# Top-k attention before two expert layers: the threshold sign takes its bias straight from the 24th maximum, and five of eight tiles are masked on VectorE instead of four

## The chip, the cores and the metric

The kernel runs on one core of one Trainium2 chip. The metric is the device time of one execution in microseconds (us); less is better. Engines are named as in the profile: PE is TensorE (PEld its weight loads), DVE is VectorE, ACT is ScalarE, POOL is GpSimd, SP is SyncE, which here only issues DMAs.

## What is computed

Attention over 4 batches, 8 heads, 576 positions and head size 64, of which each query keeps only its 32 largest scores; the result goes through a layer of three matrices with a maximum (512 to 768 to 512) and then through one of eight experts for each token (512 to 1024 to 512).

```python
scores = (1 / sqrt(64)) * q @ k.T
kth = np.partition(scores, -32, axis=-1)[..., -32:-31]
scores = np.where(scores >= kth, scores, -1e9)
attn = softmax(scores)          # exp of scores less their maximum, over their sum + 1e-9
x = (attn @ v)                  # 2304 tokens x 512
x = np.maximum(np.maximum(x @ w1, x @ w2), x @ w3) @ w_out
e = argmax(x @ w_gate, axis=1)  # one expert for each token, with its softmax weight
out[token] = weight * (np.maximum(x @ ew1[e], 0) @ ew2[e])
```

The change lies in the second and third line: how the 32nd largest score of a row is found, and how the smaller ones are dropped.

## The kernel before

The attention is cut into 144 tiles of 128 query rows by 576 scores, in 36 groups of four. The program is written out by hand in ticks: tick t holds one stage of each of some dozen tiles in flight, in a fixed order on each engine, and each engine works its own queue in that order. A tile n goes through these stages:

- PE multiplies q and k; ACT copies the scores to a tile `s`, scaled by 2^-68 (L899).
- DVE, tick n: the 8 largest of each sixth of a row (`c<-s`, L921, six instructions), then three rounds on these 48 candidates (L936 to L940). The last round leaves `T3`, whose last column is the row's 24th largest candidate. L946 multiplies this column by -(1 - 2^-21) and writes it to `bf`.
- ACT, tick n + 2: `g`, the sign of `s` plus `bf` (L968), written as an unsigned 16-bit number, with its row sum in `cnt` (how many scores lie above). Read as a half float, a 1 is 2^-24.
- POOL, tick n + 3: `f` = `s` - `g` (L974). The scores are far below 2^-24, so that those above the threshold become very small negative numbers.
- DVE, tick n + 4: the 8 largest of `f` (L983), which are the 25th to 32nd of the row. After the fourth tile of a group DVE works for all four: `hsel` from `cnt` (L989), a copy of the 24th into `y8` (L991), `heq`, a test for near ties (L992), then a product and a sum (L1012, L1013) that give `hkth`, the 32nd.
- The scores under `hkth` are then dropped in one of two ways. "Early" tiles: ACT makes a second sign against `hkth` (L1043), POOL subtracts it from `s` (L1046), and ACT's exponential `e` (L1052) gives 0 there. The others: ACT takes the exponential of all of `s`, and DVE masks `e` with s >= hkth (L1057, one instruction, whose inputs `s` and `e` both lie in SBUF).
- ACT rounds `e` to half (L1063), POOL takes the rest (L1067), a DMA transposes both, PE multiplies with v (L1086), DVE divides.

`early(n)` decides by the table `ZN`: with `ZN = (2,)` the third and fourth tile of each group are early, so that 72 tiles take each way. `let_in` makes the next POOL subtraction of `s` wait for the masks written out before it. At the end `st_verdict` counts rows without a valid `hkth` and rows with a near tie (`heq`); if any were found the whole kernel would be run again in a general form, which does not happen here.

Between these stages PE works on the two later layers with what the ticks leave: the list of work for each tick is fixed in the program. After the last tile the expert layers run on alone.

Of the kernel before, what the change touches and what calls it, by code (L numbers as in the profile page):

```python
# [7 lines left out]
F32 = mybir.dt.float32  # L8
F16 = mybir.dt.float16
I32 = mybir.dt.int32  # L10
U16 = mybir.dt.uint16
ACTF = mybir.ActivationFunctionType
ALU = mybir.AluOpType
AX = mybir.AxisListType
# [5 lines left out]
def kernel(  # L20
# [20 lines left out]
    P = 128  # L41
# [13 lines left out]

    DOWN = 2.0 ** -68
    LOW = -1.0e30
    UNIT_RATE, TAIL_RATE = 1.08, 2.0
    NEARLY, NPICK, NMIX, NS1 = 10, 2, 7, 8
    CAP, XA, NSL, NLD, NAHEAD = 1.2, 3, 10, 4, 4  # L60
    NSWAP, XLAG, KLAG, TSTOP, EARLY_RATE, LATE_RATE = 4, 2, 2, 140, 1.4, 1.8
    RANK_LAG = 1
    ZN, NFB, NGB = (2,), 2, 4
    WARM, ST = 4, 4
    ESC = 1.0 / (float(D) ** 0.5 * SC * SC * DOWN)
    LSC = 1.0 / (SC * SC)
# [28 lines left out]
    def attempt(ctx, general):  # L95
# [5 lines left out]
        tri16 = const.tile([P, P], F16, name="tri16")  # L101
        one = const.tile([P, 1], F32, name="one")
        NG = NTL // G
        bad = const.tile([P, 2], F32, name="bad")
        base = const.tile([P, NE], F32, name="base")
        ebase = const.tile([1, NE], F32, name="ebase")

# [21 lines left out]
        wg = const.tile([P, 2, KD, NE], F16, name="wg")  # L129

        def consts():
            nc.gpsimd.iota(iota32, pattern=[[0, G], [-2, 9]], base=2 * TOP - S, channel_multiplier=0,
                           allow_small_or_imprecise_dtypes=True)
            nc.gpsimd.iota(rev8, pattern=[[-1, NE]], base=NE, channel_multiplier=0,
                           allow_small_or_imprecise_dtypes=True)
            nc.gpsimd.iota(base, pattern=[[REG, NE]], base=0, channel_multiplier=0,
                           allow_small_or_imprecise_dtypes=True)
            nc.gpsimd.iota(ebase, pattern=[[REG, NE]], base=0, channel_multiplier=0,
                           allow_small_or_imprecise_dtypes=True)
            nc.vector.tensor_copy(out=viota, in_=iota32)  # L140
# [12 lines left out]
            nc.gpsimd.affine_select(out=tri16, in_=ones16, pattern=[[1, P]], compare_op=ALU.is_gt, fill=0.0,  # L153
                                    base=0, channel_multiplier=-1)
# [472 lines left out]
        with ExitStack() as p1:  # L627
# [28 lines left out]
            if not general:  # L656

                hsel = a_p.tile([P, NHS, G, 9], F16, name="hsel")
                hkth = a_p.tile([P, NG, G], F32, name="hkth")
                heq = a_p.tile([P, NG, G, 1], F16, name="heq")  # L660
            live = [0]

            def mm_tile():
# [4 lines left out]
            def freed():  # L668
                live[0] -= 1
# [207 lines left out]
                return go  # L877


            Sps, Ss, T1, T3, zz, bf, be, cnt, y8, kth, ff, ee, pt = ({} for _ in range(13))  # L880
            xhl, xrem, avt = {}, {}, {}

            def st_scores(n):
# [40 lines left out]
            def st_rounds(n):  # L924
# [14 lines left out]
                    lambda: nc.vector.match_replace(out=c, in_to_replace=t2, in_values=c2, imm_value=LOW),  # L939
                    lambda: nc.vector.max(out=T3[g][:, i], in_=c),  # L940
                ]
                if i == 0:
                    cnt[g] = sm_p.tile([P, G, 1], F32, tag="cnt", name="cnt")
                    bf[g] = sm_p.tile([P, G, 1], F32, tag="bf", name="bf")
                ops.append(None)
                ops.append(lambda: nc.vector.tensor_scalar(out=bf[g][:, i], in0=T3[g][:, i, 7:8], scalar1=-(1.0 - 2.0 ** -21),  # L946
                                                           scalar2=None, op0=ALU.mult))
                return chain(ops)

            def st_bias(g):  # L950
# [11 lines left out]
            def st_over(n):  # L962

                if general:
                    return
                g, i = divmod(n, G)
                gg[n] = wk_p.tile([P, S], U16, tag="g", name="g", bufs=NGB)
                nc.scalar.activation(out=gg[n], in_=Ss[n], func=ACTF.Sign, bias=bf[g][:, i], accum_out=cnt[g][:, i])  # L968

            def st_rest(n):  # L970
                if general:
                    return
                ff[n] = wk_p.tile([P, S], F32, tag="f", name="f", bufs=NFB)
                let_in(nc.gpsimd.tensor_tensor(out=ff[n], in0=Ss[n], in1=gg.pop(n).bitcast(F16), op=ALU.subtract))  # L974

            def st_next8(n):
                if general:
# [7 lines left out]
            def st_pick(g):  # L985

                if general:
                    return
                bulk.append(lambda: nc.vector.tensor_tensor(out=hsel[:, g % NHS], in0=viota,  # L989
                                                            in1=cnt[g].to_broadcast([P, G, 9]), op=ALU.is_equal))  # L990
                tail_bulk.append(lambda: nc.vector.tensor_copy(out=y8[g][:, :, 0:1], in_=T3[g][:, :, 7:8]))  # L991
                tail_bulk.append(lambda: nc.vector.scalar_tensor_tensor(  # L992
                    out=heq[:, g], in0=y8[g][:, :, 1:2], scalar=-1.0, in1=bf[g], op0=ALU.mult, op1=ALU.is_le))

            def st_kth(g):
                kt = sm_p.tile([P, G], F32, tag="kth", name="kth") if general else hkth[:, g]
                kth[g] = kt
                if general:
# [10 lines left out]
                        nc.vector.tensor_copy(out=kt[:, i:i + 1], in_=m8[:, 7:8])  # L1009
                    return chain([lambda i=i: search(i) for i in range(G)])  # L1010
                return chain([
                    lambda: nc.vector.tensor_tensor(out=y8[g], in0=hsel[:, g % NHS], in1=y8[g], op=ALU.mult),  # L1012
                    lambda: nc.vector.tensor_reduce(out=kt, in_=y8[g], axis=AX.X, op=ALU.add),  # L1013
                ])

            def st_verdict():

                hit = a_p.tile([P, NG * G], F16, name="hit")
                chain([
                    lambda: nc.vector.tensor_scalar(out=hit, in0=hkth.rearrange("p n g -> p (n g)"), scalar1=0.0,  # L1020
                                                    scalar2=None, op0=ALU.is_gt),
                    lambda: nc.vector.tensor_reduce(out=bad[:, 0:1], in_=hit, axis=AX.X, op=ALU.add),
                    lambda: nc.vector.tensor_reduce(out=bad[:, 1:2], in_=heq.rearrange("p n g e -> p (n g e)"),
                                                    axis=AX.X, op=ALU.add),
                    lambda: nc.vector.scalar_tensor_tensor(out=bad[:, 0:1], in0=bad[:, 0:1], scalar=-1.0,
                                                           in1=bad[:, 1:2], op0=ALU.mult, op1=ALU.add),
                ])

                def total():
                    ps = mm_tile()[0:1, 0:1]  # L1030
                    nc.tensor.matmul(out=ps, lhsT=one, rhs=bad[:, 0:1], start=True, stop=True)
                    after(1, lambda: chain([lambda: (nc.vector.tensor_scalar(
                        out=again, in0=ps, scalar1=float(P * NTL), scalar2=None, op0=ALU.add), freed())]))
                after(4, total)


# [737 lines left out]
```

## Time and profile before

| | |
|---|---|
| median of 3 runs | 921.35 us (921.21 to 921.8) |
| profiled execution | 916.4 us, span 914.7 us |
| busy share of the span | PE 81%, PEld 63%, DVE 82%, ACT 75%, POOL 65% |
| first and last mask on DVE (L1057) | starts at 73.5 and 676.6 us |
| mean granted TensorE clock | 0.964 |

Busy time is time in which at least one instruction of the engine was at work. On DVE an instruction starts before the one ahead of it has ended, so that the durations of single instructions add up to more than the busy time; where it matters the start-to-start time is taken instead, from the timeline.

### The profile page before, as it was taken

The numbers are of one execution on the slowest core, as the hardware profiler recorded it, in microseconds if no ns is written. First come the engines' busy times: TensorE is split into PE (matmuls) and PEld (weight loads), VectorE is DVE, ScalarE is ACT, GpSimd is POOL, SyncE is SP. The second block draws the span as 40 slices with busy tenths as digits, with TensorE's granted clock in tenths as the row PEclk, the third lists the DMA queues.
The fourth block names the chain that finished last, engine by engine and source line by source line (L and its number), as shares of the span: only waits on it lengthen the run. The fifth ranks groups of instructions, "written<-read, shape, count | busy, mean of one in ns | idle before, by whom it ended". The sixth has DMA issues, their size and how long they took to land.

```text
span 914.7 us, 29063 instructions
## 1 busy us (share of the span) xinstructions
PE 738.9 (81%) x10606; PEld 574.4 (63%) x10606; DVE 749.4 (82%) x3252; ACT 682.1 (75%) x1320; POOL 597.5 (65%) x554
## 2 busy tenths in 40 slices
PE   1111357888888799978988889989999999999993
PEld 0000236666665678757767687767987756687882
DVE  5999999999999899999998999999852426476661
ACT  4758899988998899899987889998862231566661
POOL 2556789898989699987877889879982220211110
PEclk9999977999899899999989999999999999999997
DMA  9872977886997998899999888897977469699280
GB/s 227 264 228 50 221 150 148 134 140 133 186 173 148 161 166 168 158 197 178 163 168 177 166 151 165 162 190 148 196 148 128 128 171 298 170 295 265 60 221 19
DMA packets 372162, 155.91 MB, mean 170 GB/s; under 512 B 331931, under 2 KB 348319, under 8 KB 372000
## 3 DMA queue, kind: packets, MB, share of 16 engines
q1 hardware_dynamic: 368128, 143.10, 76.3%
q0 software_dynamic: 3136, 9.46, 3.2%
q8 instruction: 87, 1.43, 0.7%
q10 hardware_dynamic: 736, 1.32, 0.5%
q14 instruction: 75, 0.61, 0.2%
HBM read 76.06 MB, written 16.67 MB: 101 GB/s over the span
## 4 chain that ended last, share of the span: by engine, by line
DVE 32%; issue 20%; PE 19%; POOL 11%; ACT 7%; DMA 7%; SPq 2%; POOLq 0%; DVEq 0%; ACTq 0%
PE mm L355 9%; DVE c L921 7%; DVE vec L983 4%; DVE e L1057 4%; POOL phl L1067 3%; POOL f L974 3%; PE av L1086 2%; POOL s L1046 2%; DVE a L1164 2%; DVE hl L746 1%; DMA st<-in_q_dram 1%; POOL out_dram L405 1%; ACT e L1052 1%; DVE c L937 1%; DVE c L939 1%
## 5 line engine op out<-in xcount | busy, mean ns | idle before, releaser
L355 PEld LDWEIGHTS <-W 128*128 128x128 f16 x4560 | 250.4, 100 | 22.7 <-issue 19.6
L355 PE MATMUL mm<-xT,W 128*128 128x128 f16 x3456 | 214.3, 224 | 16.0 <-DVE vl L746 4.8
L974 POOL TENSOR_TENSOR f<-s,g 128x576 f32<-128x576 f32 x144 | 184.4, 1281 | 34.5 <-ACT g L968 16.5
L1067 POOL TENSOR_TENSOR phl<-e,phl 128x576 f16<-128x576 f32 x144 | 189.0, 1313 | 8.7 <-ACT phl L1063 7.8
L921 DVE MAX8 c<-s 128x8 f32<-128x96 f32 x864 | 174.8, 243 | 3.7 <-ACT s L899 3.7
L892 PEld LDWEIGHTS <-qT 128*128 128x128 f16 (+1 forms) x640 | 56.2, 106 | 184.2 <-issue 149.1
L892 PE MATMUL S<-kt,qT 128*128 128x64 f16 (+3 forms) x320 | 60.3, 337 | 107.3 <-ACT s L899 92.1
L1052 ACT ACTIVATE e<-s,be 128x576 f32<-128x576 f32 x144 | 110.8, 769 | 23.8 <-POOL phl L1067 15.8
L1086 PE MATMUL av<-vh,pt 128*128 128x65 f16 (+3 forms) x1600 | 109.7, 199 | 15.1 <-DVE xn L1135 9.7
L983 DVE MAX8 vec<-f 128x8 f32<-128x576 f32 x144 | 108.9, 756 | 4.7 <-POOL f L974 2.0
L968 ACT ACTIVATE g<-s,bf 128x576 uint16<-128x576 f32 x144 | 111.0, 771 | 0.5 <-DVE bf L946 0.5
L1046 POOL TENSOR_TENSOR s<-s,g 128x576 f32<-128x576 f32 x72 | 92.7, 1287 | 25.4 <-DVE e L1057 24.4
L1086 PEld LDWEIGHTS <-pt 128*128 128x128 f16 (+3 forms) x2400 | 88.5, 102 | 28.0 <-issue 11.8
L899 ACT ACTIVATE s<-S 128x576 f32<-128x576 f32 x144 | 92.4, 642 | 17.9 <-PE S L892 17.7
L1063 ACT ACTIVATE phl<-e 128x576 f16<-128x576 f32 x144 | 97.3, 676 | 11.0 <-DMA pt<-phl 10.7
L1086 PE MATMUL av<-vl,pt 128*128 128x64 f16 (+3 forms) x800 | 99.3, 196 | 0.0
L461 DVE SCALAR_TENSOR_TENSOR W<-st,W 128x1024 f16<-128x1024 f32 x56 | 65.8, 1221 | 37.3 <-ACT W L460 31.8
L1057 DVE SCALAR_TENSOR_TENSOR e<-s,hkth,e 128x576 f32<-128x576 f32 x72 | 81.8, 1136 | 11.7 <-ACT e L1052 7.7
L892 PE MATMUL S<-kT,qT 128*128 128x512 f16 (+3 forms) x320 | 48.9, 295 | 18.8 <-ACT s L899 18.5
L1170 POOL TENSOR_TENSOR hhl<-a,hhl 128x384 f16<-128x384 f32 x36 | 37.0, 1027 | 33.4 <-ACT hhl L1169 31.9
L460 ACT ACTIVATE W<-st 128x1024 f16<-128x1024 f32 x56 | 55.6, 1046 | 1.8 <-DMA st<-in_moe_w_dram 1.8
L1043 ACT ACTIVATE g<-s,hkth 128x576 uint16<-128x576 f32 x72 | 55.2, 767 | 0.0
(233 smaller groups left out, 1566.6 us busy)
## 6 DMA issues: line engine op xcount, KB each, us to landing
st<-in_moe_w_dram SPq DMA_DIRECT2D x72, 512.0 KB
st<-in_moe_w_dram SPq DMA_DIRECT2D x28, 256.0 KB
raw<-in_moe_w_dram SPq DMA_DIRECT2D x12, 512.0 KB
st<-in_v_dram SPq DMA_DIRECT2D x16, 256.0 KB
hs<-he SPq DMA_DIRECT2D x16, 256.0 KB
hTe<-hs SPq DMA_DIRECT2D x8, 512.0 KB
st<-in_q_dram SPq DMA_DIRECT2D x15, 256.0 KB
qT<-qT SPq DMA_DIRECT2D x30, 128.0 KB
```

What stands on the lines that cost most here:

```text
L355: nc.tensor.matmul(out=ps[:, o * n:(o + 1) * n], lhsT=w(b, kk, c), rhs=x(a, kk), start=(kk == 0 and i == 0), stop=(kk == KD - 1 and i == 2))
L892: nc.tensor.matmul(out=ps[o:o + m, j, 0:(REM if j else NQ * P)], lhsT=qt[:, vv, hh, 0:m], rhs=kr[:, hh] if j else km[:, hh // HG, :, hh % HG],
L921: nc.vector.max(out=c[:, i * 8:(i + 1) * 8], in_=s[:, i * CW:(i + 1) * CW])
L968: nc.scalar.activation(out=gg[n], in_=Ss[n], func=ACTF.Sign, bias=bf[g][:, i], accum_out=cnt[g][:, i])
L974: let_in(nc.gpsimd.tensor_tensor(out=ff[n], in0=Ss[n], in1=gg.pop(n).bitcast(F16), op=ALU.subtract))
L983: bulk.append(lambda: nc.vector.max(out=y8[g][:, i, 1:9], in_=y))
L1046: let_in(nc.gpsimd.tensor_tensor(out=Ss[n], in0=Ss[n], in1=zz.pop(n).bitcast(F16), op=ALU.subtract))
L1052: nc.scalar.activation(out=e, in_=Ss.pop(n) if early(n) else Ss[n], func=ACTF.Exp, scale=ESC, bias=be[g][:, i])
L1057: masked.append(nc.vector.scalar_tensor_tensor(out=e, in0=Ss.pop(n), scalar=kth[g][:, i:i + 1], in1=e, op0=ALU.is_ge, op1=ALU.mult))
L1063: nc.scalar.activation(out=ph[:, 0, 0:S], in_=p, func=ACTF.Copy)
L1067: nc.gpsimd.tensor_tensor(out=ph[:, 1, 0:S], in0=p, in1=ph[:, 0, 0:S], op=ALU.subtract)
L1086: nc.tensor.matmul(out=av[o:o + m, i, 0:n], lhsT=t[0:kk, p * NCH + c, o:o + m], rhs=v_rows(x, b, c, hh)[:, 0:n], start=(c == 0 and p == 0 ...
```

## The change

Three edits. The sign that finds the scores below the 24th no longer reads `bf`: the 24th goes in as its bias as it stands, and the scores are multiplied by -(1 + 2^-22) inside the sign. A 1 now marks a score below, so POOL multiplies by it instead of subtracting: scores below are scaled by 2^-24, those above become 0. `bf` and L946 are gone, `y8` and the product are scaled to fit (L991, L1012), and the count's table of numbers is turned round. The test for near ties (`heq`, L992) and its part of the verdict are gone. And `ZN` is now (2, 1): in every second group only the fourth tile is early, and its third is masked on DVE, so that 54 tiles are early and 90 are masked.

```diff
-    ZN, NFB, NGB = (2,), 2, 4
+    ZN, NFB, NGB = (2, 1), 2, 4
...
-            nc.gpsimd.iota(iota32, pattern=[[0, G], [-2, 9]], base=2 * TOP - S, channel_multiplier=0,
+            nc.gpsimd.iota(iota32, pattern=[[0, G], [2, 9]], base=S - 2 * TOP, channel_multiplier=0,
...
-                ops.append(None)
-                ops.append(lambda: nc.vector.tensor_scalar(out=bf[g][:, i], in0=T3[g][:, i, 7:8], scalar1=-(1.0 - 2.0 ** -21),
-                                                           scalar2=None, op0=ALU.mult))
...
-                nc.scalar.activation(out=gg[n], in_=Ss[n], func=ACTF.Sign, bias=bf[g][:, i], accum_out=cnt[g][:, i])
+                nc.scalar.activation(out=gg[n], in_=Ss[n], func=ACTF.Sign, scale=-(1.0 + 2.0 ** -22),
+                                     bias=T3[g][:, i, 7:8], accum_out=cnt[g][:, i])
...
-                let_in(nc.gpsimd.tensor_tensor(out=ff[n], in0=Ss[n], in1=gg.pop(n).bitcast(F16), op=ALU.subtract))
+                let_in(nc.gpsimd.tensor_tensor(out=ff[n], in0=Ss[n], in1=gg.pop(n).bitcast(F16), op=ALU.mult))
...
-                tail_bulk.append(lambda: nc.vector.tensor_copy(out=y8[g][:, :, 0:1], in_=T3[g][:, :, 7:8]))
-                tail_bulk.append(lambda: nc.vector.scalar_tensor_tensor(
-                    out=heq[:, g], in0=y8[g][:, :, 1:2], scalar=-1.0, in1=bf[g], op0=ALU.mult, op1=ALU.is_le))
+                tail_bulk.append(lambda: nc.vector.tensor_scalar(out=y8[g][:, :, 0:1], in0=T3[g][:, :, 7:8],
+                                                                 scalar1=DROP, scalar2=None, op0=ALU.mult))
...
-                    lambda: nc.vector.tensor_tensor(out=y8[g], in0=hsel[:, g % NHS], in1=y8[g], op=ALU.mult),
+                    lambda: nc.vector.scalar_tensor_tensor(out=y8[g], in0=hsel[:, g % NHS], scalar=1.0 / DROP, in1=y8[g],
+                                                           op0=ALU.mult, op1=ALU.mult),
```

The order of PE's and SP's instructions is the same in both kernels. On DVE, one tick that closes a group (names: `hsel`, `heq` and `hkth` as above, `vec` is `y8` in PSUM, `T` are the round's maxima). Before:

```order
L983 MAX vec<-f 128x8
L939 MATCH_REPLACE c<-t_1488,c_1487 128x48
L989 TENSOR_TENSOR hsel<-vec,cnt 128x36
L940 MAX T_1363<-c 128x8
L991 COPY vec<-T_1124 128x4
L992 SCALAR_TENSOR_TENSOR heq<-vec,bf 128x4
L946 TENSOR_SCALAR bf<-T_1363 128x1
L921 MAX c<-s 128x8 x2
L1012 TENSOR_TENSOR vec<-hsel,vec 128x36
```

The same tick on DVE in the changed kernel, whose line numbers are a few lower:

```order
L980 MAX vec<-f 128x8
L939 MATCH_REPLACE c<-t_1450,c_1449 128x48
L986 TENSOR_TENSOR hsel<-vec,cnt 128x36
L940 MAX T_1331<-c 128x8
L1050 SCALAR_TENSOR_TENSOR e<-s,hkth,e 128x576
L988 TENSOR_SCALAR vec<-T_1098 128x4
L921 MAX c<-s 128x8 x2
L1008 SCALAR_TENSOR_TENSOR vec<-hsel,vec 128x36
```

The two small instructions L992 and L946 are gone, and a mask (L1057 before, L1050 now) stands in this tick, where before there was none.

On ACT, two ticks at the same group (`be` opens the next group's biases; `g,cnt` is the first sign, `g` from `hkth` the second). Before:

```order
L952 ACTIVATE be<-T_1598 128x4
L968 ACTIVATE g,cnt<-s,bf 128x576
L1043 ACTIVATE g<-s,hkth 128x576
L1063 ACTIVATE phl_149<-e 128x576
L1052 ACTIVATE e<-s,be 128x576
L899 ACTIVATE s<-S 128x576
L968 ACTIVATE g,cnt<-s,bf 128x576
L1043 ACTIVATE g<-s,hkth 128x576
L1063 ACTIVATE phl_150<-e 128x576
```

And ACT in the changed kernel, where L964 is the first sign, L1036 the second and L1045 the exponential:

```order
L946 ACTIVATE be<-T_1558 128x4
L964 ACTIVATE g,cnt<-s,T_1559 128x576
L1056 ACTIVATE phl_149<-e 128x576
L1045 ACTIVATE e<-s,be 128x576
L899 ACTIVATE s<-S 128x576
L964 ACTIVATE g,cnt<-s,T_1957 128x576
L1036 ACTIVATE g<-s,hkth 128x576
L1056 ACTIVATE phl_150<-e 128x576
L1045 ACTIVATE e<-s,be 128x576
```

The second sign of the group's third tile is gone, and that tile's exponential stands at the head of its tick (the last row), where before it stood behind that tick's copy of the scores and first sign, past these rows. On POOL the one subtraction L1046 that belonged to this tile is gone, and nothing else has moved.

## Rows read from the trace of the kernel before

**Rows 1.** Busy time of each engine by stretch: two of the attention, one after it.
```profile
core 0: us, PE busy (x) PEld busy (x) DVE busy (x) ACT busy (x) POOL busy (x), PEclk, DMA share, GB/s
350.00:400.00 50.00, 46.65 (x779) 38.19 (x776) 49.30 (x261) 46.53 (x98) 47.15 (x41) 1.00 0.88 174
550.00:600.00 50.00, 46.65 (x796) 37.65 (x793) 48.92 (x245) 46.05 (x96) 43.51 (x39) 1.00 0.88 166
650.00:700.00 50.00, 49.75 (x779) 41.06 (x776) 26.77 (x93) 29.86 (x58) 38.26 (x36) 1.00 0.95 167
```
**Rows 2.** The chain that ended last, 70 to 610 us: shares by line.
```profile
by line: DVE c L921 10.8%; issue 10.8%; DVE vec L983 7.1%; DVE e L1057 6.6%; POOL phl L1067 4.6%; POOL f L974 4.6%; PE mm L355 3.2%; POOL s L1046 2.7%; DVE a L1164 2.6%; DVE hl L746 2.2%; ACT e L1052 2.2%; DVE c L939 2.0%; DVE c L937 2.0%; 
```
**Rows 3.** The same chain, 610 to 700 us.
```profile
by line: PE mm L355 48.0%; PE av L1086 15.0%; PE S L892 5.7%; PE mm L1179 5.5%; PE mm L1181 5.3%; PE mm L1180 5.0%; PE mm L366 4.0%; PE mm L367 3.8%; PE mm L368 3.8%; DVE xr L1187 0.8%; ACT xr L1186 0.7%; PE mm L1201 0.6%; DVE xn L1135 0.5%
```
**Rows 4.** Groups on DVE: busy us, mean ns of one | idle before, releaser.
```profile
L1057 DVE SCALAR_TENSOR_TENSOR e<-s,hkth,e 128x576 f32<-128x576 f32 x72 | 81.8, 1136 | 11.7 <-ACT e L1052 7.7 <-ACT phl L1063 3.7
...
L1164 DVE TENSOR_TENSOR a<-a,mm 128x384 f32<-128x384 f32 x72 | 39.1, 543 | 16.6 <-PE mm L355 13.7 <-ACT xhl L1107 2.2
...
L746 DVE TENSOR_TENSOR hl<-mm,hl 128x512 f16<-128x512 f32 (+1 forms) x33 | 22.3, 676 | 4.4 <-ACT mm L745 4.2
L946 DVE TENSOR_SCALAR bf<-T 128x1 f32<-128x1 f32 x144 | 21.0, 146 | 1.4
...
L1135 DVE TENSOR_TENSOR xn<-av,rec 128x256 f32<-128x256 f32 x36 | 14.6, 404 | 0.2
...
L992 DVE SCALAR_TENSOR_TENSOR heq<-vec,bf 128x4 f16<-128x4 f32 x36 | 5.8, 162 | 0.9
```
**Rows 5.** Timeline of DVE, 401 to 406 us: start us, duration us.
```profile
401.05 0.21 DVE L940 MAX8 T<-c 128x8 f32<-128x48 f32 x1
401.18 0.96 DVE L739 SCALAR_TENSOR_TENSOR hl<-st,hl 128x512 f16<-128x512 f32 x1
...
402.59 0.15 DVE L991 COPY vec<-T 128x4 f32<-128x4 f32 x1
402.77 0.16 DVE L992 SCALAR_TENSOR_TENSOR heq<-vec,bf 128x4 f16<-128x4 f32 x1
402.85 0.41 DVE L921 MAX8 c<-s 128x8 f32<-128x96 f32 x2
...
405.84 0.20 DVE L940 MAX8 T<-c 128x8 f32<-128x48 f32 x1
406.08 0.15 DVE L946 TENSOR_SCALAR bf<-T 128x1 f32<-128x1 f32 x1
406.15 0.41 DVE L921 MAX8 c<-s 128x8 f32<-128x96 f32 x2
```
**Rows 6.** The line L1057 alone: durations min/median/max, and who waited for it.
```profile
L1057 DVE SCALAR_TENSOR_TENSOR e<-s,hkth,e x72: 797/1008/3120, 73.5 to 676.6; 128x576 f32<-128x576 f32 x72
...
  POOL s L1046: 24.4, 23
```
**Rows 7.** Timeline of DVE and POOL around two masks.
```profile
220.50 1.27 POOL L974 TENSOR_TENSOR f<-s,g 128x576 f32<-128x576 f32 x1
221.38 2.25 DVE L1057 SCALAR_TENSOR_TENSOR e<-s,hkth,e 128x576 f32<-128x576 f32 x1 [1.12 <-ACT e L1052]
221.74 1.27 POOL L1067 TENSOR_TENSOR phl<-e,phl 128x576 f16<-128x576 f32 x1
223.55 0.20 DVE L940 MAX8 T<-c 128x8 f32<-128x48 f32 x1
...
271.80 1.01 DVE L1057 SCALAR_TENSOR_TENSOR e<-s,hkth,e 128x576 f32<-128x576 f32 x1
272.14 1.80 POOL L1067 TENSOR_TENSOR phl<-e,phl 128x576 f16<-128x576 f32 x1
```
**Rows 8.** Groups on ACT and POOL: the exponential, the two signs, the three subtractions.
```profile
L968 ACT ACTIVATE g<-s,bf 128x576 uint16<-128x576 f32 x144 | 111.0, 771 | 0.5 <-DVE bf L946 0.5
L1052 ACT ACTIVATE e<-s,be 128x576 f32<-128x576 f32 x144 | 110.8, 769 | 23.8 <-POOL phl L1067 15.8 <-POOL s L1046 7.9
...
L1043 ACT ACTIVATE g<-s,hkth 128x576 uint16<-128x576 f32 x72 | 55.2, 767 | 0.0
...
L1067 POOL TENSOR_TENSOR phl<-e,phl 128x576 f16<-128x576 f32 x144 | 189.0, 1313 | 8.7 <-ACT phl L1063 7.8 <-POOL s L1046 0.7
L974 POOL TENSOR_TENSOR f<-s,g 128x576 f32<-128x576 f32 x144 | 184.4, 1281 | 34.5 <-ACT g L968 16.5 <-DVE T L940 6.1 <-DVE e L1057 5.7
L1046 POOL TENSOR_TENSOR s<-s,g 128x576 f32<-128x576 f32 x72 | 92.7, 1287 | 25.4 <-DVE e L1057 24.4 <-DVE nrow L234 0.7
```

More of the change, by code (lines that the diff above doesn't have):

```diff
@@ L57 @@
     LOW = -1.0e30
+    DROP = 2.0 ** -24
     UNIT_RATE, TAIL_RATE = 1.08, 2.0
@@ L103, in attempt @@
         NG = NTL // G
-        bad = const.tile([P, 2], F32, name="bad")
+        good = const.tile([P, 1], F32, name="good")
         base = const.tile([P, NE], F32, name="base")
@@ L659, in attempt @@
                 hkth = a_p.tile([P, NG, G], F32, name="hkth")
-                heq = a_p.tile([P, NG, G, 1], F16, name="heq")
             live = [0]
@@ L877, in prep_w @@
                 return go
-            Sps, Ss, T1, T3, zz, bf, be, cnt, y8, kth, ff, ee, pt = ({} for _ in range(13))
+            Sps, Ss, T1, T3, zz, be, cnt, y8, kth, ff, ee, pt = ({} for _ in range(12))
             xhl, xrem, avt = {}, {}, {}
@@ L941, in st_rounds @@
                 ]
-                if i == 0:
-                    cnt[g] = sm_p.tile([P, G, 1], F32, tag="cnt", name="cnt")
-                    bf[g] = sm_p.tile([P, G, 1], F32, tag="bf", name="bf")
-                ops.append(None)
-                ops.append(lambda: nc.vector.tensor_scalar(out=bf[g][:, i], in0=T3[g][:, i, 7:8], scalar1=-(1.0 - 2.0 ** -21),
-                                                           scalar2=None, op0=ALU.mult))
                 return chain(ops)
@@ L966, in st_over @@
                 g, i = divmod(n, G)
+                if i == 0:
+                    cnt[g] = sm_p.tile([P, G, 1], F32, tag="cnt", name="cnt")
                 gg[n] = wk_p.tile([P, S], U16, tag="g", name="g", bufs=NGB)
-                nc.scalar.activation(out=gg[n], in_=Ss[n], func=ACTF.Sign, bias=bf[g][:, i], accum_out=cnt[g][:, i])
+                nc.scalar.activation(out=gg[n], in_=Ss[n], func=ACTF.Sign, scale=-(1.0 + 2.0 ** -22),
+                                     bias=T3[g][:, i, 7:8], accum_out=cnt[g][:, i])
             def st_rest(n):
@@ L1021, in st_verdict @@
                                                     scalar2=None, op0=ALU.is_gt),
[L1022 to L1026, printed above, removed]
+                    lambda: nc.vector.tensor_reduce(out=good, in_=hit, axis=AX.X, op=ALU.add),
                 ])
@@ L1030, in total @@
                     ps = mm_tile()[0:1, 0:1]
-                    nc.tensor.matmul(out=ps, lhsT=one, rhs=bad[:, 0:1], start=True, stop=True)
+                    nc.tensor.matmul(out=ps, lhsT=one, rhs=good, start=True, stop=True)
                     after(1, lambda: chain([lambda: (nc.vector.tensor_scalar(
-                        out=again, in0=ps, scalar1=float(P * NTL), scalar2=None, op0=ALU.add), freed())]))
+                        out=again, in0=ps, scalar1=-1.0, scalar2=float(P * NTL), op0=ALU.mult, op1=ALU.add), freed())]))
                 after(4, total)
```

## The prediction

> **What bounds the kernel now.** I read the stretches first, then the chain of work that ended last, then the groups of the lines that the change touches.
>
> In the attention three engines are nearly full at once. From 350 to 400 us DVE is busy 49.30 us of 50, POOL 47.15 and ACT 46.53; from 550 to 600 us it is 48.92, 43.51 and 46.05 [rows 1]. The reader should see that DVE has least room, but that the other two are only 2 to 5 us of 50 behind it. Busy time alone then does not say what a removed instruction is worth. The chain does: from 70 to 610 us (540 us) its largest lines are DVE's maxima, but it goes over to POOL and ACT again and again. POOL's f, phl and s have 4.6, 4.6 and 2.7%, ACT's exponential 2.2%, DVE's mask 6.6% [rows 2]. From 610 us on the chain is PE almost alone [rows 3], and DVE falls to 26.77 us of 50 in 650 to 700 [rows 1]. So work saved on DVE, ACT or POOL counts until about 610 us. PE's order does not change, so behind that point everything only starts earlier by what was gained, and nothing more is to be had.
>
> **DVE, removed.** L946 runs 144 times for 146 ns, 21.0 us, and L992 36 times for 162 ns, 5.8 us [rows 4]: together 26.8 us if each duration were a slot of its own. It is not, since the next instruction starts earlier. Where L946 stands behind the maximum that it reads, it starts 0.24 us after it and gives way after 0.07 us; where L940 has another instruction behind it, that starts after 0.13 us [rows 5]. In 40 of the 144 tiles the program has L946 directly behind L940, so its slot is 0.07 us and in these 40 another 0.11: 10.1 + 4.4 = 14.5 us. L992 waits 0.18 us for the copy ahead of it and takes 0.08 us [rows 5]. A copy that nobody waits for would give way as L946 does, after 0.07, so L992 costs 0.19 us in the 26 groups where it stands directly behind the copy and 0.08 in the other 10: 5.7 us. That makes 20 us at least, 26.8 at most; I take 23, the middle. The two edits that only change an operation (L991 a product instead of a copy, L1012 with one more product in the same pass) keep their sizes of 128x4 and 128x36, and I cost them at nothing: even 0.02 us on each of the 72 would be 1.4 us.
>
> **DVE, added.** 18 more masks. The mean duration is 1136 ns [rows 4], and the next instruction starts 0.08 us before the end (223.55 against 221.38 + 2.25) [rows 7], so 1.06 us of DVE each, 19.0 us. Alone a mask takes 0.797 us, the median is 1.008 and the longest 3.120 [rows 6]. So 18 cost 18 x 0.72 = 13.0 us if nothing stands in their way, and 18 x 2.17 = 39 us if each were like the one at 221.38 us. I take the mean, because the new masks meet the same POOL work as the old ones. DVE in sum: 23 less, 19 more, 4 us less (10 at best; 16 to 19 more at worst).
>
> What stretches a mask is in rows 7. The one at 221.38 us starts while POOL's f runs (220.50 for 1.27 us), POOL's next follows without a gap, and the mask ends only after that. At 271.80 us it is the other way round: the mask is through in 1.01 us, and POOL's phl takes 1.80 us instead of the usual 1.31 [rows 7, 8]. One of the two waits for the other. [...]
>
> **ACT and POOL, removed.** 18 second signs of 767 ns, 13.8 us, and 18 subtractions of 1287 ns, 23.2 us [rows 8]. The first sign keeps its cost: L1043 already is a sign with a scale and a bias from a column, and it takes 767 ns against 771 without a scale [rows 8]. POOL's product in the place of a subtraction has no row. Below, 1281 ns is all POOL's, and nothing in the rows makes a product cheaper. On DVE product, maximum and subtraction lie on one line of sizes: 404 ns for 256 elements (product), 543 for 384 (maximum), 676 for 512 (subtraction) [rows 4]; there the operation has no price. I take the same for POOL, a change of nothing; above, only a step to twice the passes (1.28 us more, 144 times) would show, and that is a rival.
>
> New waits: a third tile's mask now waits for its exponential in the same tick (all 72 waited 7.7 us for it [rows 4], so 18 may wait 2 us), and behind it in DVE's queue stand the next tile's candidates, for which ACT's first sign waits two ticks later; that slack hides it. Fewer of POOL's subtractions wait for masks: 24.4 us in 23 waits of L1046 are there now [rows 6], and 18 of its 72 instructions go.
>
> **The sum.** I weigh each engine's saving with how often its work is on the chain up to 610 us. The mask is on it for 6.6% of 540 us, 35.6 us, of 72 x 1.06 = 76 us: 47%. So 4 us of DVE are worth 1.9 us. L1046 is on it for 2.7%, 14.6 us; a quarter of its instructions goes, 3.6 us. The exponential is on it for 2.2%, 11.9 us of 110.8 [rows 2, 8], 11%; 13.8 us of signs by the same share give 1.5 us. Sum 7.0 us. When a piece leaves the chain, the next-latest work takes part of its place (PE and the loads are unchanged), so I take 5 us, between the 1.9 of DVE alone and 7.0. The profiled execution of 916.4 us would become 911.4. It stands 0.5% under the median of the runs, 921.35; the 5 us taken from that give **916.3 us**.
>
> **The rivals.**
> 1. [...] The 18 masks land in ticks where POOL is in the way, and each costs 2.17 us as at 221.38 [rows 7]. DVE then has 39 - 23 = 16 us more, times 0.47 = 7.5, less 3.6 and 1.5: 2.4 us longer, 923.8. It decides once the mean of a new mask passes 1.88 us start to start (18 x 1.88 = 34, and (34 - 23) x 0.47 = 5.1). Against it: the median is 1.008 [rows 6] and POOL has less to do than before. Chance 0.12.
> 2. *A product on POOL is dearer than a subtraction: slower.* At twice the time POOL would have 184 us more on an engine that is 87 to 94% full, and the attention would grow by well over 100 us, to above 1020. The DVE line of rows 4 speaks against it. Chance 0.04.
> 3. *Nothing moves.* The small instructions were cover for other waits, and DVE's saving goes into waiting for loads and PE; the time stays within 0.2%, about what a measurement of this kernel can tell from no change: 921.3. For it: "issue" is 10.8% of the chain, time in which no work is shown [rows 2]. Chance 0.17.
> 4. *More than I count.* POOL, with 23 us less to do, stands in the way of fewer masks, all 90 come nearer 0.797 us, and the 18 cost 13.0: DVE 10 us less, 4.7 on the chain, with 3.6 and 1.5 and no discount 9.8 us: 911.5. Chance 0.12.
>
> **How the numbers follow.** The forecast, 2 to 8 us less, has 0.55. Faster by over 0.2% (under 919.5) are the forecast and rival 4, 0.67; within 0.2% rival 3, 0.17; slower rivals 1 and 2, 0.16. The range goes from a little past rival 4, 910.5, to just under rival 1, 923.0, which leaves out about 1 in 10 above and less below.
>
> **What would show it.** Right: the group of `bf` gone, 90 masks of 1.0 to 1.15 us mean, 54 second signs and 54 of POOL's `s`, f's product near 1.28 us, POOL some 20 us less busy, ACT 14, DVE 2 to 6, the last mask at about 671 us in place of 676.6, and the stretch behind it as long as now. Wrong: masks over 1.5 us mean (rival 1), f over 1.4 us (rival 2), the last mask at 676 with more idle DVE in front of it (rival 3), or PE's stretch behind 610 us longer than before at a lower clock, which nothing in this sum holds.

## The result, and the profile after

The changed kernel takes 925.24 us, the median of 6 runs (923.33 to 927.13), against 920.72 us of 6 runs of the kernel before on the same chips (918.68 to 921.8): a ratio of 1.0061 [1.0043, 1.0079]. It is slower by 0.5 to 0.6%, about 5 us (the medians alone give 1.0049), where 5 us less were forecast. The profiled execution, the fastest of the six, took 923.33 us; its span is 921.6 us and its mean granted clock 0.973, higher than before. The other five had 0.956 to 0.964, so this trace alone does not clear the clock; runs 10 and 12 below do.

Busy time in two stretches of the attention, as in [rows 1], of the changed kernel:

```profile
350.00:400.00 50.00, 45.90 (x780) 37.96 (x777) 48.56 (x237) 44.95 (x94) 43.66 (x40) 1.00 0.93 173
550.00:600.00 50.00, 46.69 (x811) 37.82 (x808) 47.60 (x219) 43.54 (x90) 42.05 (x37) 1.00 0.88 161
```

The chain that ended last, 70 to 610 us, as in [rows 2]:

```profile
by line: DVE c L921 10.7%; PE mm L356 9.7%; issue 8.9%; DVE vec L980 6.9%; DVE e L1050 6.0%; PE av L1079 3.0%; PE S L892 2.8%; ACT e L1045 2.6%; POOL phl L1060 2.4%; ACT s L899 2.4%; POOL f L971 2.3%; ACT g L964 2.0%; DVE c L937 1.9%; DVE c
```

The groups that answer to [rows 4, 8] (L964 is the first sign, L1036 the second, L1045 the exponential, L1050 the mask, L971, L1060 and L1039 are POOL's f, phl and s):

```profile
L1060 POOL TENSOR_TENSOR phl<-e,phl 128x576 f16<-128x576 f32 x144 | 187.4, 1301 | 11.7 <-ACT phl L1056 11.6
L971 POOL TENSOR_TENSOR f<-s,g 128x576 f32<-128x576 f32 x144 | 184.3, 1280 | 52.2 <-ACT g L964 24.7 <-DVE T L940 15.4 <-DVE e L1050 4.7
L964 ACT ACTIVATE g<-s,T 128x576 uint16<-128x576 f32 x144 | 110.9, 770 | 0.0
L1045 ACT ACTIVATE e<-s,be 128x576 f32<-128x576 f32 x144 | 110.6, 768 | 17.9 <-POOL phl L1060 13.0 <-POOL s L1039 4.7
L1050 DVE SCALAR_TENSOR_TENSOR e<-s,hkth,e 128x576 f32<-128x576 f32 x90 | 97.1, 1079 | 15.7 <-ACT e L1045 15.6
L1039 POOL TENSOR_TENSOR s<-s,g 128x576 f32<-128x576 f32 x54 | 69.4, 1286 | 24.6 <-DVE e L1050 19.2 <-DVE vec L988 2.6 <-ACT g L1036 1.1
L1036 ACT ACTIVATE g<-s,hkth 128x576 uint16<-128x576 f32 x54 | 41.4, 767 | 0.0
```

And the line of the mask alone, as in [rows 6]:

```profile
L1050 DVE SCALAR_TENSOR_TENSOR e<-s,hkth,e x90: 786/900/3118, 73.5 to 685.4; 128x576 f32<-128x576 f32 x90
```

Nothing here is dear. The masks are shorter on average than before (1079 ns against 1136), the product takes what the subtraction took (1280 against 1281), the new sign 770 against 771. In the stretches of the attention all three engines are *less* busy than before. DVE's maxima and masks keep their share of the chain; POOL's f, phl and s fall from 4.6, 4.6 and 2.7% to 2.3 and 2.4% with s no longer shown, and PE's L356 (L355 before) rises from 3.2 to 9.7%. The reader should see what the groups cannot tell: POOL's idle time before f grew from 34.5 to 52.2 us, ACT saved 18 signs, and still the work came later. By the timelines the start of a tile's `vec` (L980; L983 before) agrees within 1.5 us until tile 51, then lies 0.3 to 3.6 us later, mostly about 2, comes nearly level at tile 120 (0.2) and is 4.2 us later at the last tile.

### The profile page after: what moved, and what is told of

Its sections match the earlier page's. It is cut to its first block, busy times and chain, and to the rows that moved or that the text cites. A ratio compares the mean times of both kernels' runs of the same rounds, so it can differ in the third digit from the quotient of the medians.

```text
span 921.6 us, 28947 instructions
## 1 busy us (share of the span) xinstructions
PE 740.9 (80%) x10606; PEld 574.4 (62%) x10606; DVE 747.9 (81%) x3088; ACT 671.6 (73%) x1302; POOL 579.0 (63%) x536
## 4 chain that ended last, share of the span: by engine, by line
DVE 32%; PE 24%; issue 18%; ACT 8%; POOL 7%; DMA 6%; SPq 2%; POOLq 0%; DVEq 0%; ACTq 0%
PE mm L356 12%; DVE c L921 8%; DVE vec L980 5%; DVE e L1050 4%; PE av L1079 3%; PE S L892 2%; ACT e L1045 2%; DVE bits L866 1%; ACT s L899 1%; POOL phl L1060 1%; DVE bits L863 1%; PE mm L1172 1%; POOL out_dram L406 1%; DMA xs<-xr,si 1%; POOL f L971 1%
## 5 line engine op out<-in xcount | busy, mean ns | idle before, releaser
L356 PEld LDWEIGHTS <-W 128*128 128x128 f16 x4560 | 248.4, 100 | 21.0 <-issue 18.2
L356 PE MATMUL mm<-xT,W 128*128 128x128 f16 x3456 | 212.5, 223 | 16.2 <-DVE hl L746 6.7
L971 POOL TENSOR_TENSOR f<-s,g 128x576 f32<-128x576 f32 x144 | 184.3, 1280 | 52.2 <-ACT g L964 24.7
L1060 POOL TENSOR_TENSOR phl<-e,phl 128x576 f16<-128x576 f32 x144 | 187.4, 1301 | 11.7 <-ACT phl L1056 11.6
L921 DVE MAX8 c<-s 128x8 f32<-128x96 f32 x864 | 175.2, 243 | 8.5 <-ACT s L899 4.2
L1045 ACT ACTIVATE e<-s,be 128x576 f32<-128x576 f32 x144 | 110.6, 768 | 17.9 <-POOL phl L1060 13.0
L980 DVE MAX8 vec<-f 128x8 f32<-128x576 f32 x144 | 108.8, 755 | 4.4 <-POOL f L971 0.9
L1056 ACT ACTIVATE phl<-e 128x576 f16<-128x576 f32 x144 | 97.3, 676 | 19.4 <-DMA pt<-phl 19.2
L964 ACT ACTIVATE g<-s,T 128x576 uint16<-128x576 f32 x144 | 110.9, 770 | 0.0
L1050 DVE SCALAR_TENSOR_TENSOR e<-s,hkth,e 128x576 f32<-128x576 f32 x90 | 97.1, 1079 | 15.7 <-ACT e L1045 15.6
L1039 POOL TENSOR_TENSOR s<-s,g 128x576 f32<-128x576 f32 x54 | 69.4, 1286 | 24.6 <-DVE e L1050 19.2
L356 PEld LDWEIGHTS <-W1e 128*128 128x128 f16 x864 | 48.9, 98 | 5.4 <-issue 2.5
```

Source lines behind the costliest of these rows:

```text
L356: nc.tensor.matmul(out=ps[:, o * n:(o + 1) * n], lhsT=w(b, kk, c), rhs=x(a, kk), start=(kk == 0 and i == 0), stop=(kk == KD - 1 and i == 2))
L921: nc.vector.max(out=c[:, i * 8:(i + 1) * 8], in_=s[:, i * CW:(i + 1) * CW])
L964: nc.scalar.activation(out=gg[n], in_=Ss[n], func=ACTF.Sign, scale=-(1.0 + 2.0 ** -22), bias=T3[g][:, i, 7:8], accum_out=cnt[g][:, i])
L980: bulk.append(lambda: nc.vector.max(out=y8[g][:, i, 1:9], in_=y))
L1045: nc.scalar.activation(out=e, in_=Ss.pop(n) if early(n) else Ss[n], func=ACTF.Exp, scale=ESC, bias=be[g][:, i])
L1050: masked.append(nc.vector.scalar_tensor_tensor(out=e, in0=Ss.pop(n), scalar=kth[g][:, i:i + 1], in1=e, op0=ALU.is_ge, op1=ALU.mult))
```

## The experiments

Each ratio is to runs of the kernel before on the same chip, with its 95% interval. Runs 1 to 4 shared one chip, runs 5 to 8 a second, 9 to 12 a third and 13 to 18 a fourth (17 and 18 later than the others). My first theory was that the fifth mask costs more than I had taken and the sign gains; the first rival, that the sign or the product cost. Later theories are named in the expectations.

**1. The sign without the table.**

```diff
-    ZN, NFB, NGB = (2, 1), 2, 4
+    ZN, NFB, NGB = (2,), 2, 4
```


> The changed kernel with the old table, ZN = (2,): the sign without a bias column, the product on POOL, no near-tie test, and 72 masks as before. Theory A (the 18 moved tiles cost more than they give, and the sign is a small gain): DVE loses about 7 us of slots that were not hidden (104 signs' thresholds of 0.07 us) and 5 us around the near-tie test, of which about half counts, so 4 to 7 us faster than before, 914 to 917 us, and the last mask some 5 us earlier. Theory B (the sign itself costs, the table does not): 3 to 6 us slower than before, like the whole change. Theory C (both are nothing alone, the loss is in their meeting): within 2 us of before.

919.98 us (12 runs), 1.0046 [1.0027, 1.0064]. The first theory's gain is not there: without any new mask the change is slower too. By the start of `vec` it is about 1 us ahead between tiles 10 and 77 and 4.0 us behind at the last.

**2. The table without the sign.** The kernel before with `ZN = (2, 1)`.

```diff
-    ZN, NFB, NGB = (2,), 2, 4
+    ZN, NFB, NGB = (2, 1), 2, 4
```


> The kernel before with ZN = (2, 1) and nothing else: the threshold column, the subtraction and the near-tie test stay, 90 tiles are masked on VectorE. Theory A: 18 masks of 0.8 to 1.06 us come on top of a VectorE that is 97% full, and the saving on ScalarE and GpSimd is not on the path: 8 to 14 us slower than before, 929 to 935 us. Theory B: within 2 us of before. Theory C: within 2 us of before.

923.09 us (6 runs), 1.0078 [1.0057, 1.01]. The table costs, though less than expected.

**3 and 4. A third buffer for `c`,** in the changed kernel and in run 1's. With L946 gone, L921 of the next tile stands directly behind L940 in 39 tiles and writes the buffer that L940 reads; a third buffer frees it from that wait.

```diff
-                c = sm_p.tile([P, CAND * 8], F32, tag="c", name="c", bufs=2)
+                c = sm_p.tile([P, CAND * 8], F32, tag="c", name="c", bufs=3)
```


> The changed kernel with a third buffer for the candidates c (bufs=3 instead of 2). In the changed kernel the first maximum L921 of a tile waits for the last maximum L940 in front of it, since it writes the buffer that L940 reads; it starts 0.29 to 0.32 us behind it, as late as when the threshold instruction stood between them. Theory D (this inherited wait is where the saving of the 40 threshold instructions went): L921 starts 0.12 to 0.13 us behind L940, 40 times 0.18 = 7 us of VectorE are freed, and the time falls by 3 to 7 us against the changed kernel, to 918 to 922 us. Rival: something else holds L921 (the scores from ScalarE), the spacing stays 0.3 us, and the time stays at 925 us within 1.5.

> The sign alone (old table, ZN = (2,)) with the third buffer for c: the version that should be best if theories A and D both hold. A and D: 3 to 7 us faster than the sign alone, 7 to 13 us faster than before, 908 to 914 us. If only A holds: as the sign alone. If neither: slower than before.

921.31 us (8 runs), 1.0055 [1.0035, 1.0075], and 920.55 us (12 runs), 1.0041 [1.0019, 1.0063]. No gain over the changed kernel (on other chips) and over run 1 that the intervals tell. The wait is real, as L921 now follows L940 after 0.15 us on average in place of 0.31, but it is not where the time went.

**5. The sign with the old stream.** Run 1 with `bf` and `heq` computed again, and used by nobody.

```diff
+                if i == 0:
+                    bf[g] = sm_p.tile([P, G, 1], F32, tag="bf", name="bf")
+                ops.append(None)
+                ops.append(lambda: nc.vector.tensor_scalar(out=bf[g][:, i], in0=T3[g][:, i, 7:8], scalar1=-(1.0 - 2.0 ** -21),
+                                                           scalar2=None, op0=ALU.mult))
...
+                tail_bulk.append(lambda: nc.vector.scalar_tensor_tensor(
+                    out=heq[:, g], in0=y8[g][:, :, 1:2], scalar=-1.0, in1=bf[g], op0=ALU.mult, op1=ALU.is_le))
```


> The sign alone (old table), but VectorE's two small instructions are put back with results that nobody uses: the threshold column (144 times) and the near-tie test (36 times), so that VectorE's order is that of the kernel before. The sign alone was 0.46% slower than before although VectorE had less to do. Theory E (the freed slots themselves shift masks against GpSimd, and the masks get dearer: 1186 ns mean there against 1133): with the slots filled again the time is that of before within 0.2%, and the masks are back near 1133 ns. Theory F (the new sign, the product on GpSimd or their operands cost): it stays 0.3 to 0.6% slower than before, as the sign alone, or more.

918.32 us (12 runs), 1.0007 [0.9986, 1.0028]. The sign and the product cost nothing. Adding 180 useless instructions took away run 1's loss: either free slots hurt, or something else came back with them.

**6. A blank: the kernel before with the third buffer** (the edit of runs 3 and 4). Nothing waits for it there, and the order of instructions is that of the kernel before.

> The kernel before with a third buffer for the candidates c: the order of every engine is the same, and L921 had no wait on L940 there, since the threshold instruction stood between them. A blank that only moves tiles in SBUF. Theories E and F: within 0.2% of before. Rival G (the kernel answers to any shift of addresses or of chance by some 0.4%): 0.3% or more off to either side, and then the other small differences would tell little.

920.41 us (12 runs), 1.0027 [1.0007, 1.0047]. A blank that is slower: the third buffer also moves the tiles behind it by 192 bytes.

**7. The kernel before without the tie test.**

```diff
-                heq = a_p.tile([P, NG, G, 1], F16, name="heq")
...
-                tail_bulk.append(lambda: nc.vector.scalar_tensor_tensor(
-                    out=heq[:, g], in0=y8[g][:, :, 1:2], scalar=-1.0, in1=bf[g], op0=ALU.mult, op1=ALU.is_le))
```


> The kernel before without the near-tie test (36 instructions L992 and their part of the verdict); the rest is as before. It leaves out the check for near ties. Priced by slots it frees 36 times 0.08 to 0.19 us of VectorE, 3 to 7 us, of which half would count: 1.5 to 3 us faster. Theory E: no faster, within 0.2%, or up to 0.3% slower, as freed slots turn into waits. Theory F: 1.5 to 3 us faster.

916.31 us (12 runs), 0.9989 [0.9968, 1.001]. The tie test is left out, and its 36 instructions are worth nothing that can be measured.

**8. The changed kernel without the order between masks and POOL.**

```diff
-                while masked:
-                    tc.add_manual_dep(ins.ins, masked.pop().ins.name,
-                                      mybir.DependencyInfo(mybir.DependencyClass.Sync, mybir.DependencyReason.SCHED_ONLY),
-                                      reason="the mask reads through GpSimd's port")
+                masked.clear()
```


> The changed kernel without the order between masks and GpSimd: let_in adds no wait, so GpSimd's subtractions of s no longer wait for the masks written out before them (no data passes between them). Theory H (the change costs because GpSimd, whose next f or s waits for 18 more masks, is held up: waits on masks 19.2 + 4.7 us and more booked on L940, 15.4): these waits vanish and the time falls 3 to 8 us below the changed kernel, to before or under it. Theory L (the port itself is the cost): masks then start against busy GpSimd work, their mean rises over 1.2 us, and the time stays at the changed kernel's or is up to 6 us longer.

933.23 us (6 runs), 1.0169 [1.0138, 1.0201]. Its groups of f and of the mask (L968 and L1047 there):

```profile
L968 POOL TENSOR_TENSOR f<-s,g 128x576 f32<-128x576 f32 x144 | 196.2, 1362 | 66.7 <-ACT g L961 42.9 <-DVE vec L977 14.8 <-DVE vl L746 1.6
L1047 DVE SCALAR_TENSOR_TENSOR e<-s,hkth,e 128x576 f32<-128x576 f32 x90 | 114.8, 1276 | 13.3 <-ACT e L1042 13.0
```

Theory L holds, and the loss is larger than it allowed: some 10 us over the changed kernel by the two ratios. Without the order a mask takes 1276 ns in place of 1079, and f 1362 in place of 1280. The two engines hold each other up as in [rows 7], and the order that `let_in` makes keeps this cheap. The wait of f for the masks in the changed kernel is thus a price paid for something dearer. That a port is what they meet at, as the expectation and the code's comment have it, was not shown: the runs show the durations and the time.

**9 to 12. Is it the instructions, or where the tiles lie?** By the addresses in the built programs, dropping `bf` moved every tile behind it down by 96 bytes, and dropping `heq` moved the scores and all behind them by 288 more. Runs 9 and 10 are run 1 and the changed kernel with this storage reserved and left empty; run 11 is the kernel before with 192 empty bytes; run 12 is the changed kernel once more.

```diff
+                a_p.tile([P, NG, G, 1], F16, name="heq")
...
+                    sm_p.tile([P, G, 1], F32, tag="bf", name="bf")
```
```diff
+            kvl.tile([P, 48], F32, name="pad")
             kt0 = kvl.tile([P, H * S], F16, name="kt0")
```


> The new sign and product with four masked tiles of eight, and neither the bias nor the tie test computed, as in the run with the sign alone; but the storage of the two is still reserved and left empty, so that every tile in SBUF lies at the address that it has in the kernel before. (Dropping the storage moved every tile behind it down by 96 bytes, the scores and all behind them by 384.) Theory S (slots: the loss of the sign alone, 1.0046 of the kernel before, comes from the free slots of VectorE: its masks come earlier, stand more often beside a GpSimd operation, and VectorE waits for ScalarE instead): nothing changes, 1.003 to 1.006 of the kernel before, masks of 1180 to 1220 ns, VectorE's wait for e near 14 us. Theory D (addresses: the loss comes from where the tiles lie): 0.997 to 1.001, masks near 1140 ns.

> The whole changed kernel with the storage of bias and tie test reserved and left empty, so that all other tiles lie where they lie in the kernel before. Theory S: as the changed kernel beside it, 1.005 to 1.008 of the kernel before. Theory D: 0.3 to 0.5% below the changed kernel beside it, 1.001 to 1.004 of the kernel before, since the fifth mask still costs.

> The kernel before with 192 empty bytes ahead of the first large tile, so that the weights, the scores and all behind them lie 192 bytes higher, as they did with the third buffer, but with no third buffer; the instructions and their order are those of the kernel before. Theory S (and chance in the run with the third buffer): 0.998 to 1.002 of the kernel before. Theory D: 1.002 to 1.005, the same as the kernel before with the third buffer (1.0027).

> The changed kernel itself once more, on the same chip as the three others, as the measure for the one with the layout kept: 1.004 to 1.008 of the kernel before by either theory.

0.999 [0.9969, 1.0011], 1.0012 [0.9991, 1.0034], 1.0044 [1.0025, 1.0064] and 1.0045 [1.0028, 1.0062] (medians 920.62, 920.85, 924.7 and 924.4 us, 12 runs each, against 920.49). By the times theory D holds in all four: with the tiles where they were, most of the loss is gone, and empty bytes alone make the kernel before as slow as the changed one. The masks of run 9 went theory S's way: 1192 ns, where theory D had some 1140 (run 1 has 1186, run 5 1142). The free slots do go with longer masks, but no loss of time goes with these. Two stretches of the kernel before, then the same of run 11, which has the same instructions:

```profile
250.00:450.00 200.00, 175.71 (x2611) 139.77 (x2610) 191.77 (x971) 181.83 (x371) 172.79 (x150) 0.97 0.91 168
450.00:660.00 210.00, 193.11 (x3041) 159.35 (x3039) 195.11 (x973) 183.44 (x375) 177.42 (x157) 0.97 0.91 168
```
```profile
250.00:450.00 200.00, 174.89 (x2532) 138.88 (x2531) 189.10 (x954) 178.44 (x363) 169.11 (x147) 0.94 0.91 163
450.00:660.00 210.00, 191.50 (x2927) 156.55 (x2925) 192.94 (x955) 179.88 (x368) 171.62 (x150) 0.94 0.90 165
```

In equal time DVE, ACT and POOL did 1 to 3% less, and the DMA engines, as busy as before (0.91 and 0.90), moved 163 and 165 GB/s in place of 168. That points to a transfer. PE's granted clock is lower in these stretches (0.94 against 0.97); over the span and all executions it is 0.959 in run 11 and 0.965 in the kernel before. But runs 12 and 10 have 0.964 and 0.965 and still lie 3.6 us apart, so the clock does not explain the loss.

**13 to 16. Which tile?** The packets of 256 bytes show it; they are those of the transposes, and 144 of the 259 transposes are `pt<-phl`. Their times fall into two kinds over all runs so far, and the kinds go with where the three `phl` buffers start, the source of `pt<-phl`. Run 13 moves `phl` and all behind it; run 14 moves the weights too, but `phl` by 256; run 15 is the changed kernel with 96 empty bytes ahead of `phl`, which puts `phl` back and leaves the weights 96 and the scores 288 bytes lower; run 16 is run 2 again.

```diff
+            a_p.tile([P, 48], F32, name="pad2")
             phl = [a_p.tile([P, 2, SPAD], F16, name=f"phl{i}") for i in range(NPH)]
```


> The kernel before with 192 empty bytes directly ahead of the three phl buffers (the source of the transposes): they start 64 bytes off a multiple of 128, and all tiles behind them move with them; the weights and all tiles ahead stay. Theory P (the loss comes from phl off a multiple of 128 bytes): 1.003 to 1.006 of the kernel before, share of the first DMA queue near 77%, 90th percentile of the packets of 256 bytes 24 to 25 ns. Theory W (it comes from the weights, or another tile ahead of phl): 0.998 to 1.002, share near 75.5%, 18 ns.

> The kernel before with 192 empty bytes ahead of the first large tile, as in the run that lost 0.44%, and 64 more ahead of phl, so that phl starts on a multiple of 128 again; the weights stay 192 bytes higher and all tiles behind phl 256 bytes higher. Theory P: 0.998 to 1.002 of the kernel before, 18 ns. Theory W: 1.003 to 1.006, 24 to 25 ns.

> The whole changed kernel, without the storage of bias and tie test, and 96 empty bytes ahead of phl, so that phl starts on a multiple of 128 bytes as in the kernel before; the weights stay 96 bytes lower, the scores and all behind them 288. Theory P: 1.000 to 1.003 of the kernel before, as where the whole layout was kept (1.0012), 18 ns. Theory W: 1.004 to 1.007, as the changed kernel, 24 ns.

> The table alone once more (five masked tiles of eight, sign with its bias, all tiles where they lie in the kernel before), on the chip of the three others. If its first figure holds, 1.005 to 1.009 of the kernel before, and the instructions dropped with the bias give back some 5 us of it; if the gap to the layout kept (1.0012) was one of chips, 1.001 to 1.004, and they give back 2 us at most.

1.0041 [1.002, 1.0062], 0.9998 [0.9979, 1.0016], 1.0026 [1.0011, 1.004] and 1.0058 [1.0035, 1.008] (922.04, 917.63, 919.75 and 922.53 us against 917.81). Theory P holds by the times. Neither the weights (run 14 and 15) nor the scores and the tiles behind them (moved by 288 in runs 7 and 15) matter; `phl` does. No run moves `phl` without the tiles behind it, but where these start does not go with the two kinds: `pt`, which the transposes write, starts on a multiple of 256 in the changed kernel and 128 bytes behind one in the kernel before. In run 13 the packets came out near what was expected (26 ns at the 90th percentile), the share of the queue (76.6%, before 76.3%) did not.

**17 and 18. What the freed slots are worth on clean ground.** Run 1 and run 4 with empty bytes ahead of `phl` (96 and 32).

> The new sign and product with four masked tiles of eight, neither bias nor tie test computed or stored, and 96 empty bytes ahead of phl, so that phl starts on a multiple of 128 bytes as in the kernel before. Theory P with slots that are worth little: 0.997 to 1.001 of the kernel before, 18 ns at the 90th percentile. If the slots are worth what the sum of the prediction gave them (18 us of VectorE less the 2 us that lay on the chain per 4, thus some 8 us): 0.990 to 0.994.

> The same with a third buffer for c, so that the first instruction of the next tile no longer waits for the one before it, and phl on a multiple of 128 bytes. If the wait ate the credit: 0.5 to 1% below the run beside it. If the slots that it frees are only idle time elsewhere: the same as the run beside it within 0.2%.

916.69 us, 0.9986 [0.9968, 1.0004], and 921.01 us, 1.0047 [1.0031, 1.0064] (12 runs each, against 917.04). Run 17 settles the slots. Stretch 86 to 667 us of the kernel before, then of run 17:

```profile
86.00:667.00 581.00, 492.38 (x7391) 395.74 (x7390) 551.39 (x2719) 519.90 (x1059) 503.20 (x435) 0.95 0.89 166
```
```profile
86.00:667.00 581.00, 493.15 (x7377) 396.09 (x7376) 542.21 (x2548) 519.01 (x1055) 501.85 (x434) 0.95 0.87 166
```

DVE is busy 9.2 us less, and PE, ACT and POOL have done the same work as before. The 9.2 us have become idle time. Its groups of the maxima (before, then in run 17) and of the mask (run 17; before in [rows 4]) show where:

```profile
L921 DVE MAX8 c<-s 128x8 f32<-128x96 f32 x864 | 174.8, 243 | 3.7 <-ACT s L899 3.7
L922 DVE MAX8 c<-s 128x8 f32<-128x96 f32 x864 | 175.4, 243 | 12.8 <-ACT s L900 8.5
L1051 DVE SCALAR_TENSOR_TENSOR e<-s,hkth,e 128x576 f32<-128x576 f32 x72 | 84.9, 1179 | 13.0 <-ACT e L1046 12.8
```

Before the maxima DVE is now idle for 12.8 us in place of 3.7, 8.5 of it until ACT's scores. Before the masks it is idle for 13.0 in place of 11.7, and nearly all of that, 12.8 in place of 7.7, is now until ACT's exponentials. The masks last 43 ns longer each. Run 18 was meant to be on clean ground and was not: its `phl` starts on a multiple of 128 bytes, but not of 256, and its packets are of the slow kind. So the boundary is not 128 bytes, as I had it, but 256, as far as these starts go; what the third buffer is worth with `phl` in place was not measured.

All kernels with traces, by where `phl` starts (bytes behind a multiple of 256) and by the share of the 310,784 packets of 256 bytes that took over 18 ns:

```
start  kernel (ratio), share over 18 ns
0      before .084; run 2 (1.0078) .081; 5 (1.0007) .078; 7 (0.9989) .087; 9 (0.999) .084;
       10 (1.0012) .085; 14 (0.9998) .080; 15 (1.0026) .083; 16 (1.0058) .084; 17 (0.9986) .084
96     run 3 (1.0055) .149; 4 (1.0041) .151
128    run 18 (1.0047) .152
160    changed .149; run 12 (1.0045) .146; 1 (1.0046) .146; 8 (1.0169) .146
192    run 6 (1.0027) .168; 11 (1.0044) .166; 13 (1.0041) .169
```

## Why the prediction was wrong

Two terms of its sum failed, and one that it should have held was missing.

**The missing term: where the tiles lie.** The prediction followed instructions and never the storage that goes with them. The dropped buffers put `phl` 160 bytes behind a multiple of 256, and this costs 3.6 us in the changed kernel (run 12 against run 10, 924.4 to 920.85): most of the 4.5 us between the medians of the result. A start of 192 costs 0.41 and 0.44% in the kernel before (runs 13 and 11, 4.2 us by the medians). The traces agree on which starts are slow: from a start of 0, .078 to .087 of the packets of 256 bytes took over 18 ns, from the other four .146 to .169. The share is highest at 192 (.166 to .169), but it does not rise from 96 to 160 (.149 to .151, .152, .146 to .149), and 83% or more of the packets take 18 ns at most in every case. Why more packets take longer from these starts no run shows. None of the groups shown above takes longer. The mean packet went from 24.62 to 25.15 ns, 310,784 x 0.53 / 16 = 10 us on each of the 16 DMA engines if they share it evenly (an estimate); these are 0.89 busy in the attention of the kernel before. By which wait this reaches the end stays open: ACT's wait for `pt<-phl` to free a buffer rose from 10.7 to 19.2 us in the changed kernel, but it is 10.9 and 8.0 in runs 11 and 13. What was shown is only that the time goes with the start of `phl`.

**The step "DVE, removed", with its share in "The sum".** 23 us of DVE at 47% were 10.8 us, 1.2%. Alone, with `phl` in place, the removal gives 0.1% (runs 9 and 17: 0.999 and 0.9986, neither told apart from 1). Beside the fifth mask, where DVE is tighter, it gives 0.3% (run 15 against run 16, 919.75 to 922.53 us). Two things went wrong. The slots were smaller: in run 17 DVE is 9.2 us less busy in the attention, some 12 us if the longer masks (84.9 us against 81.8) are set aside. In 39 tiles the removal of L946 freed no time at all, as a place of the changed kernel shows (start us, duration us):

```profile
408.17 0.21 DVE L940 MAX8 T<-c 128x8 f32<-128x48 f32 x1
408.48 0.42 DVE L921 MAX8 c<-s 128x8 f32<-128x96 f32 x2
```

From L940 to L921 it is 0.31 us without L946, and with it 406.15 - 405.84 = 0.31 as well [rows 5]: the wait for L940 passed to the next instruction, where the prediction had it start 0.13 us after L940. And the share of the chain is not a price. DVE holds the chain because it runs in step with ACT, POOL and the transfers; freed, it waits for ACT (run 17).

**The terms for ACT and POOL in "The sum".** A quarter of L1046 and 18 signs were credited with 3.6 + 1.5 us. Busy time of each engine over the span, before and then in the changed kernel:

```profile
PE 738.9 (81%) x10606; PEld 574.4 (63%) x10606; DVE 749.4 (82%) x3252; ACT 682.1 (75%) x1320; POOL 597.5 (65%) x554
PE 740.9 (80%) x10606; PEld 574.4 (62%) x10606; DVE 747.9 (81%) x3088; ACT 671.6 (73%) x1302; POOL 579.0 (63%) x536
```

POOL is 18.5 us less busy and ACT 10.5, and both went idle: in f's row the wait for g rose from 16.5 to 24.7 us, and the one put down to L940 from 6.1 to 15.4. That one is the wait for a mask, which ends just before L940 does; in run 8, without the order, it is 0.8 us.

**"DVE, added"** was too dear if anything: the masks' mean is 1079 ns, and between tiles 8 and 120 the slots of 70 masks, start to start, sum to 68.5 us where those of 56 summed to 57.7. That is 0.77 us for each of the 14 more, against 1.06 taken, and it is rival 4's condition. The new wait for the exponentials, put at 2 us, stayed small too: DVE is idle for 11.8 us before the masks of run 2, where it was 11.7. But with the two credits gone the masks stand alone. By the prediction's terms the table was worth 8.9 - 5.1 = 3.8 us more, 0.41%; measured are 0.78% (run 2) and 0.58% (run 16), 5 to 7 us. The size was missed a little at most, as 0.41% lies inside run 16's interval; that the relief which did not come makes the difference is argued, not shown.

**The rivals.** Rival 1 ended on the right side for a reason that did not occur, as no mask mean came near 1.88 us. Rival 2 fell (1280 ns). Rival 3 names what run 17 shows, DVE's saving going into waits, though they are for ACT and not for loads and PE. Of the signs of a wrong forecast none came as written: no longer masks, no dearer f, and the last mask at 685.4 us and not 676. Most signs of a right one came, though: 90 masks of 1079 ns, 54 signs and 54 subtractions, f at 1280 ns, POOL 18.5 us less busy. They tell what the engines were given to do, not what that is worth, and a list that holds only instructions could not name a transfer.

**What is left.** With `phl` in place the changed kernel is at 1.0012 and 1.0026 (runs 10 and 15), the second slower than before. The forecast gain of 5 us would not have come without the side effect either, though the miss would have been smaller. No kernel here beats the kernel before by more than its interval; run 17, at 0.9986, comes nearest.

## What to carry to other kernels

A removed buffer moves every tile behind it: compare addresses before a small loss is put down to the instructions, and keep the source of a frequent transpose on a multiple of 256 bytes, where it was fastest here by some 0.4% of the kernel; a blank (same instructions, other addresses) shows the size of this effect. Where three engines and the transfers run in step, the share of the chain that one of them holds says who is last, not what a microsecond off it is worth. A removed instruction can leave its wait to the next one: here L921 overwrites the buffer that L940 reads, and it started 0.31 us after L940 with L946 between them and without.

## What the runs showed of the hardware that was not expected

Where the buffers of a frequent transposing DMA's source start goes with whether 8% or 15 to 17% of the 256-byte packets take over 18 ns: 8% on a multiple of 256 bytes, more from 96, 128, 160 and 192 bytes behind one. The weights ahead and the scores behind lay 96 to 288 bytes elsewhere without effect (runs 7, 14 and 15). The start is worth some 0.4% of this kernel. A mask and POOL's operations that are left to meet freely cost 1.1% (run 8 against the changed kernel, 1.0169 and 1.0061, on different chips) with fewer dependences.
